# Attention's logits in four visits a half chunk instead of five, and two changes of order in the linear layers

## The chip, the cores and the metric

One Trainium2 chip, one of its NeuronCores. A core has five engines that run side by side and wait for each other through semaphores: TensorE (PE in the profile, with its weight loads as PEld), VectorE (DVE), ScalarE (ACT), GpSimd (POOL) and SyncE (SP), which only starts DMAs here. The metric is the time of one execution on the device, in microseconds, as the median of several runs.

## The reference

Four layers over `x` of 2048 tokens by 512 features, in float32: A, B, A, B, each with a layer norm ahead and a residual add behind. There are 32 heads of 16 features.

```python
def A(x):                        # linear attention with learned features
    q, k, v = heads(layernorm(x) @ wqkv)
    phi = lambda t: concat(softmax(t @ w_phi), softmax(-(t @ w_phi)))
    o = phi(q) @ (phi(k).T @ v) / (phi(q) @ phi(k).sum(0) + 1e-6)
    return x + merge(o) @ wo

def B(x):                        # softmax attention in 4 segments of 512, with a memory
    for s in range(4):
        p = softmax(qs @ ks.T * scale + causal_mask)
        o = g * (elu1(qs) @ M / (elu1(qs) @ z + 1e-6)) + (1 - g) * (p @ vs)
        M, z = M + elu1(ks).T @ vs, z + elu1(ks).sum(0)
    return x + merge(o) @ wo
```

## The kernel before

**Number format.** Most products with weights are made of three matmuls of a rounded high part and a low part of each operand (`mm3`: high by high, high by low, low by high). The low part is a subtraction on DVE (now and then on POOL) after ACT has copied the high part.

**Layer A** has two passes over the tokens. `pass1` walks four segments of 512 tokens in the order 1, 2, 3, 0 (`SEGS`). For each it normalizes, projects `v` (`v_tile`, 16 steps of three 512-wide matmuls), and then for four tiles of 128 tokens each makes keys (`kproj`) and queries (`qproj`). A key tile's features take `extremes` (DVE), `differences` (POOL), `exp` (ACT), and `scale_k` (DVE sums, then DVE and POOL multiply); `kv` sums the outer products of features and values on PE into `mx` and `my`. The value tiles of the next segment are steps of a plan that is woven into the projections of this one. In the last segment the queries stay on the chip: `begun(t)` does their extremes and differences. `pass2` goes over the 16 query tiles. For tile `i` it transposes the last output on PE (`turn`, split by ACT into `oh` and by DVE into `ol`), takes the exponential of tile `i + 2`, multiplies tile `i` with the state `KN`, divides (`weigh`, DVE), transposes tile `i + 1`, scales tile `i + 2` (`scale_q`: DVE sums and ratio `rr`, then POOL multiplies), makes the differences of tile `i + 3` (POOL) and projects tile `i - 1` with the output weights (`out_proj`, whose end is a DVE add into `x`, shown as `xr` or `ot`).

**Layer B** is a chain of 32 half chunks (4 segments, 4 chunks of 8 heads, 2 halves of 4 heads). `steps` walks a counter `k`; half chunk `m` has `R = 5` values of it, called visits 0 to 4 here. In every visit PE does, in this order: one part of the logits of half chunk `m` (`attend`, into `lg`, two banks of PSUM with one buffer), one part of the maxima's logits of a half chunk ahead (`maxima`, into the banks `mx` and `my`), in visits 0 and 2 one half of the products of the last half chunk's probabilities with the values (`weighted`, into a bank of its own, `pv`), and then background work from a table (`FIRST`, `GAPS`, `LAST`, `FINAL`): projections, memory, transposes and output projections, all through three banks called `g`. Visits 0 and 2 have no matmuls in the tables.

The logits contract over 63 or 64 rows, so each matmul uses one half of the array's rows (`tile_position` (0, 0) or (64, 0)), for one head pair `e` = 0 or 1. In the version before, each product is issued for `e = 0` and then for `e = 1` with the same width, so the two halves of the array always carry equal pairs. The products with the values use four column strips of 32 at once. Everything else uses the whole array. By width, a half chunk's `attend` is five visits with pairs of 512, 512, 256 + 384, 256 + 384 and 256 + 256 columns; `maxima` has five groups with pairs of 256 + 384, 512, 256 + 384, 256 + 256 and 512.

After `attend` ACT takes the exponential of the whole `lg` tile (1024 columns) into a `P4` tile, and POOL zeroes the masked part of the diagonal blocks. After `maxima` DVE adds the mask and takes the row maximum of each block (16 a half chunk, each followed by a read of its accumulator). ACT scales `pv` into `U`; POOL and DVE finish later.

**Order.** The order on every engine is the order of the program: the helper `held` chains PE's instructions, and `Ordered` those of the others. The table's "~" puts the DVE subtraction or add off to the next visit, behind that visit's maxima. The waits between engines come from tiles: a bank or buffer that is written anew waits for its last readers.

The profile gives all PE matmuls line L185 and all transposes L189 (helpers), and the other engines' operations L163.

Of the kernel before, what the change touches and what calls it, by code (L numbers as in the profile page):

```python
# [11 lines left out]
ALU = mybir.AluOpType  # L12
# [19 lines left out]
PV = 1  # L32
G = 3
R = 5
FILL = (1, 3, 4)
LEAD = 9
FINAT = 8
PAUSE, DONE = object(), object()
LEFT = 24900
BEGIN = -25  # L40
MAXIMA = -9
# [9 lines left out]

FIRST = """
0.1 max k2/2       | 0.2 v3/2          | 0.3 k2~
0.4 v3             | 1.1 max m0 q3/2   | 1.3 fin q3~       | 1.4 t1 k3/1
2.1 max m1 k3      | 2.3 fin ln~       | 2.4 ln~ ln~
3.3 fin q0+/2      | 3.0 w
3.1 max ln~        | 3.4 q0+~ t2
4.1 max k0+/2 load | 4.3 fin k0+/1     | 4.4 k0+ m2
5.0 n              | 5.3 fin q1+/2 n
5.1 max v0+        | 5.4 q1+~ t3  # L60
6.1 max a0+ v1+    | 6.2 n             | 6.3 a0+ fin k1+/2
6.4 k1+ m3         | 7.0 n             | 7.2 n
7.1 max q2+~       | 7.3 fin v2+/2 n   | 7.4 v2+ t0+
"""
GAPS = """
0.2 n              | 0.3 a1 fin v3/3 n
0.1 max a1 k2~     | 0.4 v3 turn~ m0
1.0 n              | 1.2 n
1.1 max q3~        | 1.3 fin out/2     | 1.4 out t1 turn~
2.1 max a2 m1 k3~  | 2.3 fin ln out/3  | 2.4 out turn~ ln  # L70
3.1 max ln ln out~ | 3.3 a2 fin q0+/2  | 3.4 q0+~ t2
4.1 max k0+~ a3 turn~ load | 4.3 a3 fin out/3 | 4.4 out~ m2
5.0 n              | 5.3 fin v0+/2 n N
5.1 max q1+~ begin | 5.4 v0+ t3
6.0 N              | 6.1 max a0+ k1+~  | 6.2 n
6.3 a0+ fin v1+/3 N | 6.4 v1+ m3       | 7.0 n N
7.1 max q2+~       | 7.2 n N           | 7.3 fin v2+/2 n N
7.4 v2+ t0+
# [3 lines left out]
0.1 max a1 k2~     | 0.2 n             | 0.3 a1 fin v3/3 n  # L82
1.0 n              | 0.4 v3 turn~      | 1.2 n
1.1 max q3~        | 1.3 fin out/2     | 1.4 out turn~
2.1 max k3~        | 2.3 fin a2 out/2  | 2.4 out a2 turn~
3.1 max ln~ ln~    | 3.3 fin out/2 ln~ | 3.4 out ln~ turn~
4.1 max v/2        | 4.3 fin out/2     | 4.4 out v
5.1 max v/2        | 5.3 fin v         | 5.4 a3 pre
6.1 max v/2        | 6.3 fin v a3      | 6.4 v/2 pt~
7.1 p v pt~        | 7.3 fin v/2 p pt  | 7.4 v p pt  # L90
"""
FINAL = """
0.1 max k2~        | 0.3 fin v3/3      | 0.4 v3 a1
1.1 max a1 q3/2    | 1.3 fin q3~       | 1.4 turn~
2.1 max k3/2       | 2.3 fin k3        | 2.4 out/2
3.1 max a2 out turn~ | 3.3 fin out/2   | 3.4 out~ a2
4.1 max a3 turn~   | 4.3 fin out/2     | 4.4 out/1 a3
5.1 max out turn~  | 5.3 fin out/2     | 5.4 out/1 pre
6.1 max out~       | 6.3 fin           | 6.4 pt~
7.1 p pt~          | 7.3 fin p pt      | 7.4 p pt  # L100
"""
BEFORE = {-25: "q0 load", -23: "v0", -21: "k0",
          -18: "n", -17: "v1 n", -16: "n", -15: "n n", -14: "q1 n", -13: "n", -12: "k1 n", -11: "n", -10: "v2 n",
          -4: "max q2~", -1: "t0"}
# [3 lines left out]
def interleave_kernel(ctx, tc, x_in, a_wqkv, a_wphi, a_wo, b_wq, b_wk, b_wv, b_wo, b_beta,  # L108
# [479 lines left out]
    class LayerA:  # L588
# [68 lines left out]
        def pass1(self, first):  # L657
# [35 lines left out]
            for n, s in enumerate(SEGS):  # L693
# [51 lines left out]
                if n < NSEG - 1:  # L745
# [5 lines left out]
                    plan += [(j, vt) for j in vals]  # L751
# [82 lines left out]
                begun(3)  # L834
# [9 lines left out]
        def pass2(self):  # L844
# [22 lines left out]
            for i in range(NT + 1):  # L867
# [5 lines left out]
                if i < NT:  # L873
# [24 lines left out]
                if 0 < i < 3:  # L898
                    yield from transposed(i + 1)
                x = ahead  # L900


    class LayerB:
        def __init__(self, xsrc, xdst):
            self.xsrc, self.xdst = xsrc, xdst
            self.st, self.hT, self.vv, self.ot, self.mx, self.U = {}, {}, {}, {}, {}, {}
            self.pr, self.pv = {}, {}
            self.later, self.late, self.rows, self.turned = [], [], [], []
# [109 lines left out]
        def maxima(self, m):  # L1018


            s, c, hf = m // 8, m % 8 // 2, m % 2
# [3 lines left out]
            def prod(pb, r, i, at, w):  # L1025
                for e in range(2):
                    q, k = Q[64 * e : 64 * e + 63, r, :], K[64 * e : 64 * e + 63, r, :]
                    mm(pb[e][:, at : at + w], lhsT=q[:, i * P : (i + 1) * P], rhs=k[:, 0:w],
                       start=True, stop=True, tile_position=(64 * e, 0))

            def top(pb, e, r, i, at):
                n = (i + 1) * P
                col = (e * 2 + r) * 4 + i
                pl = pb[e][:, at : at + n]
# [5 lines left out]
            for what in ([(0, 0, 0), (0, 2, P)], [(0, 3, 0)], [(1, 0, 0), (1, 2, P)],  # L1040
                         [(0, 1, 0), (1, 1, 256)], [(1, 3, 0)]):
                pb = [PS(t, 1) for t in ("mx", "my")]
                for r, i, at in what:
                    prod(pb, r, i, at, max(256, (i + 1) * P))
                for e in range(2):
                    for r, i, at in what:
                        top(pb, e, r, i, at)
# [12 lines left out]
        def attend(self, m):  # L1060


            s, c, hf = m // 8, m % 8 // 2, m % 2
# [3 lines left out]
            def prod(pb, r, kb, at, w):  # L1067
                for e in range(2):
                    q, k = Q[64 * e : 64 * e + 64, r, :], K[64 * e : 64 * e + 64, r, :]
                    mm(pb[:, e, at : at + w], lhsT=k[:, kb * P : (kb + 1) * P],  # L1070
                       rhs=q[:, 512 - w : 512], start=True, stop=True, tile_position=(64 * e, 0))

            for kbs, r in (((0,), 0), ((0,), 1), ((1, 3), 0), ((1, 3), 1), ((2,), None)):
                pb = PS("lg", 1, (P, 2, 512))
                pr = T2("P4", NP4, shape=(P, 2, 512))
                pq = pr.rearrange("p e (b x) -> p e b x", b=4)
                if kbs == (0,):
                    prod(pb, r, 0, 0, 512)
                    diags = [pr[:, :, 0:P]]
                elif kbs == (1, 3):  # L1080
                    prod(pb, r, 3, 256, 256)
                    prod(pb, r, 1, 0, 384)
                    diags = [pq[:, e, 0:4:3, :] for e in range(2)]
                else:
                    for rr in range(2):
                        prod(pb, rr, 2, 256 * rr, 256)
                    diags = [pr.rearrange("p e (r x) -> p (e r) x", r=2)[:, :, 0:P]]
                self.pr[m][kbs, r] = pr
                with tc.high_priority():
                    act.activation(pr, pb, AF.Exp, scale=0.25)  # L1090
                for diag in diags:
                    pool.affine_select(out=diag, in_=diag, pattern=[[0, diag.shape[1]], [1, P]],
                                            compare_op=ALU.is_ge, fill=0.0, base=0, channel_multiplier=-1)
                yield

        def weighted(self, m, last):
# [3 lines left out]
            if not last:  # L1100
                self.pv[m] = PS("pv", PV)
            pv, pr = self.pv[m], self.pr[m]
            for kb in ((1, 2) if last else (0, 3)):
                for r in range(2):
                    for e in range(2):
                        hh = 2 * r + e
                        h = c * 8 + hf * 4 + hh
                        if kb == 0:
                            p = pr[(0,), r][:, e, :]
                        elif kb == 2:  # L1110
                            p = pr[(2,), None][:, e, 256 * r : 256 * r + 256]
                        else:
                            p = pr[(1, 3), r][:, e, 0:384] if kb == 1 else pr[(1, 3), r][:, e, 384:512]
                        mm(pv[32 * hh : 32 * hh + 32, kb * P : 512],
                           lhsT=v[:, kb, h * VW : h * VW + 32], rhs=p,
                           start=(kb == 0), stop=(kb == 2), tile_position=(0, 32 * hh))
            if last:
                self.pr.pop(m)
                U = T2("U", 2)
                act.activation(U, self.pv.pop(m), AF.Identity, scale=share[:, m % 8 : m % 8 + 1])  # L1120
                self.U[m] = U

# [68 lines left out]
        def steps(self, side, after, table_end):  # L1191
# [75 lines left out]
            for k in range(BEGIN, R * N + 4):  # L1267
# [11 lines left out]
                if k % R in (0, 2) and 0 <= k // R - 1 < N:  # L1279
                    self.weighted(k // R - 1, k % R == 2)  # L1280
# [90 lines left out]
```

## Time and profile before

| what | value |
|---|---|
| median of three runs | 1522.89 us (1522.32 to 1524.72) |
| the profiled execution | 1523.71 us, span 1521.9 us |
| PE busy | 1456.3 us, 96% of the span |
| DVE busy | 1095.3 us, 72% |
| ACT busy | 787.1 us, 52% |
| POOL busy | 650.3 us, 43% |
| granted TensorE clock, mean | 0.995 |

Matmuls are pipelined: each is recorded for longer than it holds the array, so the records of neighbours overlap and PE looks busy through short stalls. What a matmul costs is read from the starts: the time from its start to the start of the next. A row of the timeline has the start, the length, the engine, the line, the operation, output and inputs with their shape, the count of merged instructions, and in brackets the idle time of the engine before it and what ended it.

### The profile page before, as it was taken

What the parts mean: (1) busy time and instruction counts of PE and PEld (TensorE: products, weight loads), DVE (VectorE), ACT (ScalarE), POOL (GpSimd) and SP (SyncE); (2) the same over time, 40 slices, a digit from 0 to 9 for tenths busy, and PEclk for the clock granted to TensorE, in tenths of its full rate; (3) what the DMA queues carried; (4) which work ended last, traced back from release to release, by engine and by line L of the source; (5) the groups of instructions that cost most, each with busy time, mean ns of one, the idle gap of its engine ahead of it and who ended that gap; (6) DMA issues with size and microseconds to landing.
All of it is one profiled execution on the core that took longest, in us unless ns stands there. A gap on an engine that the chain in (4) does not pass through costs nothing.

```text
span 1521.9 us, 30316 instructions
## 1 busy us (share of the span) xinstructions
PE 1456.3 (96%) x10888; PEld 1033.4 (68%) x10888; DVE 1095.3 (72%) x3258; ACT 787.1 (52%) x1178; POOL 650.3 (43%) x1000
## 2 busy tenths in 40 slices
PE   7999989999999999999999998999999999999998
PEld 6877767765666666666667786776656666666554
DVE  4765868668778877878656667757688788787783
ACT  5554335436565566556544333443565656655553
POOL 1668654313454544433314445541344445444331
PEclk9999999999999999999999999999999999999999
DMA  5487265545444443535340122744463353443340
GB/s 183 129 289 254 70 210 165 167 119 153 122 110 117 135 104 103 157 99 147 114 143 33 39 84 80 225 148 144 113 175 106 105 153 99 111 118 98 80 112 36
DMA packets 108773, 195.85 MB, mean 129 GB/s; under 512 B 14416, under 2 KB 27856, under 8 KB 107856
## 3 DMA queue, kind: packets, MB, share of 16 engines
q1 hardware_dynamic: 107472, 193.38, 42.8%
q8 instruction: 88, 1.44, 0.4%
q10 hardware_dynamic: 1152, 0.52, 0.1%
q14 instruction: 61, 0.50, 0.1%
HBM read 101.05 MB, written 39.85 MB: 93 GB/s over the span
## 4 chain that ended last, share of the span: by engine, by line
PE 78%; DVE 12%; ACT 4%; issue 2%; POOL 2%; DMA 1%; SPq 0%; ACTq 0%; POOLq 0%; DVEq 0%
PE g L185 45%; PE pv L185 9%; PE lg L185 9%; PE g L189 7%; PE mx L185 5%; PE my L185 3%; DVE mx L163 2%; POOL P L163 2%; DVE es L163 2%; ACT P L163 1%; DVE my L163 1%; DVE mxs L163 1%; ACT tb L163 1%; DVE hl L163 1%; DVE ol L163 1%
## 5 line engine op out<-in xcount | busy, mean ns | idle before, releaser
L163 ACT ACTIVATE P<-lg 128x1024 f32<-128x1024 f32 x320 | 328.9, 1028 | 173.0 <-PE lg L185 165.5
L163 POOL TENSOR_SCALAR_AFFINE_SELECT P<-P 128x256 f32<-128x256 f32 (+1 forms) x448 | 190.7, 440 | 442.3 <-ACT P L163 441.7
L163 DVE CUSTOM_DVE_ANT_0 mx<-mx,mask 128x128 f32<-128x128 f32 (+3 forms) x512 | 255.3, 499 | 160.7 <-PE my L185 109.0
L163 DVE CUSTOM_DVE_ANT_0 my<-my,mask 128x128 f32<-128x128 f32 (+3 forms) x512 | 265.9, 519 | 6.5
L185 PE MATMUL g<-hh,wqk 128*128 128x512 f32 x512 | 180.5, 407 | 2.1 <-ACT hh L163 1.4
L185 PE MATMUL lg<-e,e 64*128 64x256 f32 (+2 forms) x1024 | 168.4, 387 | 7.8 <-ACT P L163 7.6
L185 PE MATMUL g<-w,oh 128*128 128x512 f32 x512 | 170.6, 414 | 3.5 <-DVE ol L163 1.6
L185 PE MATMUL pv<-P,v 128*32 128x512 f32 (+3 forms) x2048 | 165.0, 441 | 0.0
L185 PE MATMUL my<-e,e 63*128 63x256 f32 (+2 forms) x512 | 146.7, 346 | 5.3 <-DVE mxs L163 3.9
L185 PEld LDWEIGHTS lg<-e,e 64*128 64x128 f32 x1024 | 81.1, 184 | 103.2 <-issue 50.6
L185 PE MATMUL g<-w,hh 128*128 128x512 f32 x448 | 145.8, 406 | 0.9 <-ACT tb L163 0.9
L163 DVE DVE_READ_ACCUMULATOR2_ANT mxs<- 128x1 f32 x1024 | 145.0, 142 | 0.0
L185 PE MATMUL mx<-e,e 63*128 63x256 f32 (+2 forms) x512 | 140.8, 330 | 0.2
L185 PEld LDWEIGHTS pv<-P,v 128*32 128x32 f32 x2048 | 53.7, 109 | 100.9 <-issue 92.0
L185 PEld LDWEIGHTS g<-hh,wqk 128*128 128x128 f32 x512 | 96.3, 188 | 24.0 <-ACT hh L163 1.8
L185 PEld LDWEIGHTS g<-w,oh 128*128 128x128 f32 x512 | 89.4, 190 | 30.9 <-issue 5.7
L185 PE MATMUL g<-w,ol 128*128 128x512 f32 x256 | 101.8, 398 | 0.0
L185 PE MATMUL g<-hl,wqk 128*128 128x512 f32 x256 | 100.4, 392 | 0.4 <-DVE hl L163 0.4
L163 POOL TENSOR_SCALAR tb<-tb 128x512 f32<-128x512 f32 x48 | 71.5, 1489 | 67.4 <-ACT tb L163 67.4
L163 ACT CAST ta<-g 128x512 fp32r<-128x512 f32 x64 | 37.6, 587 | 112.5 <-PE g L185 112.2
L185 PEld LDWEIGHTS my<-e,e 63*128 63x128 f32 x512 | 82.0, 185 | 18.1 <-DVE mxs L163 8.8
L185 PEld LDWEIGHTS mx<-e,e 63*128 63x128 f32 x512 | 89.7, 186 | 6.1 <-issue 3.6
(143 smaller groups left out, 2816.8 us busy)
## 6 DMA issues: line engine op xcount, KB each, us to landing
e<-ta SPq DMA_DIRECT2D x384, 128.0 KB
wqk<-wqk SPq DMA_DIRECT2D x64, 512.0 KB
x<-x SPq DMA_DIRECT2D x48, 256.0 KB
ot<-in SPq DMA_DIRECT2D x28, 256.0 KB
pq<-tb SPq DMA_DIRECT2D x24, 256.0 KB
tb<-pq SPq DMA_DIRECT2D x24, 256.0 KB
x<-xr SPq DMA_DIRECT2D x24, 256.0 KB
xr<-x SPq DMA_DIRECT2D x24, 256.0 KB
```

The source lines that it names most:

```text
L163: i = f(*a, **k)
L185: return held(nc.tensor.matmul(*a, **k))
L189: return held(nc.tensor.transpose(*a))
```

## The change

**Four visits (`R = 4`).** `attend` now has one visit for each pair (`r`, `e`). In it, head pair `e` gets its 512-wide product of key block 0, and the other pair `f = 1 - e` its 256-wide and 384-wide products of blocks 3 and 1; the array halves thus carry different widths, issued as `f` 256, `e` 512, `f` 384. Visits 2 and 3 add block 2 of pair `e` for both `r`: two 256-wide products into a new bank `mz`, with an exponential of their own. Per half chunk the matmuls are the same 16, the exponentials become six (four of 1024 columns, two of 512) instead of five, the mask operations ten instead of seven. `maxima` has four groups: three blocks (`f` 256, `f` 384, `e` 512) in two visits and five (two more 256-wide products of `e`, in `mz`) in the other two; visits 0 and 1 have the five. The 16 reductions stay. `weighted` does all 16 matmuls of a half chunk in visit 0, in one of the three `g` banks; the bank `pv` is gone and is now `mz`. The tables keep their cells, moved from visits 1, 3 and 4 to visits 1, 2 and 3; `LEAD`, `FINAT`, `BEGIN`, `MAXIMA` and `BEFORE` are moved to match, and the visits ahead of the first logits that have maxima alone are seven instead of nine.

**First linear pass.** For the last segment only, half of the 16 value steps stay in the plan of the segment before; the other eight are taken two by two after each of its four key projections (`rest`).

**Second linear pass.** `begun(3)` moves from the end of `pass1` into tile 0 of `pass2`. For each tile the differences of `i + 3` are issued ahead of the scaling of `i + 2`, and for the first three tiles the scaling moves to the end of the tile, behind the output projection.

```diff
-R = 5
+R = 4
...
-                    plan += [(j, vt) for j in vals]
+                    plan += [(j, vt) for j in (vals if n + 2 < NSEG else vals[::2])]
...
+                    rest = vt if n + 2 == NSEG else None
...
+                    for _ in range(2 if t < 4 else 0):
+                        next(rest)
+                        yield
...
-                begun(3)
+                self.begun = begun
...
-                    if i + 2 < NT:
-                        scale_q(self.e[i + 2])
+                    if i == 0:
+                        self.begun(3)
                     if i + 3 < NT:
                         self.e[i + 3] = differences(*self.raw.pop(i + 3))
+                    if 2 < i < NT - 2:
+                        scale_q(self.e[i + 2])
                     self.load_q(i + 4)
...
                 if 0 < i < 3:
                     yield from transposed(i + 1)
+                if i < 3:
+                    scale_q(self.e[i + 2])
...
-            for what in ([(0, 0, 0), (0, 2, P)], [(0, 3, 0)], [(1, 0, 0), (1, 2, P)],
-                         [(0, 1, 0), (1, 1, 256)], [(1, 3, 0)]):
+            for r, e, three in ((0, 1, True), (0, 0, False), (1, 1, False), (1, 0, True)):
                 pb = [PS(t, 1) for t in ("mx", "my")]
...
+                parts = [(pb[1 - e], 1 - e, r, 0, 0), (pb[1 - e], 1 - e, r, 2, P), (pb[e], e, r, 3, 0)]
+                if three:
+                    pz = PS("mz", 1)
+                    parts.insert(0, (pz, e, 0, 1, 0))
+                    parts.insert(2, (pz, e, 1, 1, 256))
...
+            for r in range(2):
+                for e in range(2):
+                    f = 1 - e
+                    pb = PS("lg", 1, (P, 2, 512))
...
+                    prod(pb[:, f, 256:512], f, r, 3, 256)
+                    prod(pb[:, e, :], e, r, 0, 512)
+                    prod(pb[:, f, 0:384], f, r, 1, 384)
+                    exp_of(pr, pb, pr[:, e : e + 1, 0:P], pr.rearrange("p e (b x) -> p e b x", b=4)[:, f, 0:4:3, :])
+                    if r > 0:
+                        pz = PS("mz", 1)
...
+                        for rr in range(2):
+                            prod(pz[:, 256 * rr : 256 * rr + 256], e, rr, 2, 256)
...
-            if not last:
-                self.pv[m] = PS("pv", PV)
+            pv, pr = PS("g", G), self.pr.pop(m)
+            for kb in (0, 3, 1, 2):
...
-                if k % R in (0, 2) and 0 <= k // R - 1 < N:
-                    self.weighted(k // R - 1, k % R == 2)
+                if k % R == 0 and 0 <= k // R - 1 < N:
+                    self.weighted(k // R - 1)
```

More of the change, by code (lines that the diff above doesn't have):

```diff
@@ L52 @@
 FIRST = """
[L53 to L63, printed above, removed]
+0.0 v3/2
@@ L79 @@
+7.3 v2+ t0+
 """
 LAST = """
[L82 to L90, printed above, removed]
+0.1 max a1 k2~ n   | 0.2 a1 fin v3/3 n
@@ L95 @@
[L95 to L100, printed above, removed]
-"""
-BEFORE = {-25: "q0 load", -23: "v0", -21: "k0",
-          -18: "n", -17: "v1 n", -16: "n", -15: "n n", -14: "q1 n", -13: "n", -12: "k1 n", -11: "n", -10: "v2 n",
-          -4: "max q2~", -1: "t0"}
+0.1 max k2~        | 0.2 fin v3/3      | 0.3 v3 a1
@@ L1023, in maxima, with prod @@
             mx = T2("mxs", 2, shape=(P, 16))
[L1025 to L1029, printed above, removed]
+            def prod(pb, e, r, i, at):
+                w = max(256, (i + 1) * P)
+                q, k = Q[64 * e : 64 * e + 63, r, :], K[64 * e : 64 * e + 63, r, :]
+                mm(pb[:, at : at + w], lhsT=q[:, i * P : (i + 1) * P], rhs=k[:, 0:w],
+                   start=True, stop=True, tile_position=(64 * e, 0))
             def top(pb, e, r, i, at):
@@ L1038, in top @@
                         op0=ADD, op1=MAX, accum_out=mx[:, col : col + 1])
-            for what in ([(0, 0, 0), (0, 2, P)], [(0, 3, 0)], [(1, 0, 0), (1, 2, P)],
-                         [(0, 1, 0), (1, 1, 256)], [(1, 3, 0)]):
+            for r, e, three in ((0, 1, True), (0, 0, False), (1, 1, False), (1, 0, True)):
                 pb = [PS(t, 1) for t in ("mx", "my")]
[L1043 to L1047, printed above, removed]
+                parts = [(pb[1 - e], 1 - e, r, 0, 0), (pb[1 - e], 1 - e, r, 2, P), (pb[e], e, r, 3, 0)]
[3 more added lines that the diff above has]
+                    parts.insert(2, (pz, e, 1, 1, 256))
+                for part in parts:
+                    prod(*part)
+                if not three:
+                    parts = [parts[i] for i in (0, 2, 1)]
+                for part in parts:
+                    top(*part)
                 self.mx[m] = mx
@@ L1065, in attend, with prod, exp_of @@
             self.pr[m] = {}
[L1067 to L1088, printed above, removed]
+            def prod(out, e, r, kb, w):
+                q, k = Q[64 * e : 64 * e + 64, r, :], K[64 * e : 64 * e + 64, r, :]
+                mm(out, lhsT=k[:, kb * P : (kb + 1) * P],
+                   rhs=q[:, 512 - w : 512], start=True, stop=True, tile_position=(64 * e, 0))
+            def exp_of(pr, pb, *diags):
                 with tc.high_priority():
@@ L1266, in steps @@
             spent = 0.0
-            for k in range(BEGIN, R * N + 4):
+            for k in range(BEGIN, R * N + 1):
                 m = k // R + 3
```

101 lines of the change are left out of this document (61 added, 40 removed).

## The prediction

> **What bounds the kernel now.** I read the page first (busy time, the chain that ended last), then the busy times of one stretch inside layer B, then the timeline of PE around single visits.
>
> ```profile
> PE 1456.3 (96%) x10888; PEld 1033.4 (68%) x10888; DVE 1095.3 (72%) x3258; ACT 787.1 (52%) x1178; POOL 650.3 (43%) x1000
> ...
> PE 78%; DVE 12%; ACT 4%; issue 2%; POOL 2%; DMA 1%; SPq 0%; ACTq 0%; POOLq 0%; DVEq 0%
> ...
> L163 DVE CUSTOM_DVE_ANT_0 mx<-mx,mask 128x128 f32<-128x128 f32 (+3 forms) x512 | 255.3, 499 | 160.7 <-PE my L185 109.0
> L163 DVE CUSTOM_DVE_ANT_0 my<-my,mask 128x128 f32<-128x128 f32 (+3 forms) x512 | 265.9, 519 | 6.5
> L163 DVE DVE_READ_ACCUMULATOR2_ANT mxs<- 128x1 f32 x1024 | 145.0, 142 | 0.0
> ```
>
> ```profile
> 340.00:700.00 360.00, 356.15 (x2637) 235.96 (x2636) 283.73 (x1020) 217.50 (x311) 159.90 (x287) 1.00 0.44 120
> ```
>
> The columns of the last row are the stretch, its length, and busy time of PE, PEld, DVE, ACT and POOL, then clock and DMA. PE is busy for 356 of 360 us and holds 78% of the chain; DVE follows with 284 of 360. So PE's order of work sets the time, and DVE is near enough to catch it for moments. What PE spends outside its streaming is in the starts:
>
> ```profile
> 701.83 0.40 PE L185 MATMUL g<-w,ol 128*128 128x512 f32 x1
> 702.16 0.50 PE L185 MATMUL lg<-e,e 64*128 64x256 f32 x4
> 702.50 0.28 PE L185 MATMUL mx<-e,e 63*128 63x256 f32 x1
> ...
> 702.62 0.27 PE L185 MATMUL mx<-e,e 63*128 63x256 f32 x1
> ...
> 702.82 0.73 PE L185 MATMUL g<-w,oh 128*128 128x512 f32 x2
> 703.39 0.40 PE L185 MATMUL g<-w,ol 128*128 128x512 f32 x1
> 703.62 0.64 PE L185 MATMUL g<-w,oh 128*128 128x512 f32 x2
> ...
> 705.32 0.50 PE L185 MATMUL lg<-e,e 64*128 64x512 f32 x2
> 705.66 0.40 PE L185 MATMUL mx<-e,e 63*128 63x512 f32 x1
> ...
> 705.99 1.28 PE L185 MATMUL pv<-P,v 128*32 128x512 f32 x16
> 707.21 0.50 PE L185 MATMUL lg<-e,e 64*128 64x512 f32 x2
> 707.55 0.28 PE L185 MATMUL mx<-e,e 63*128 63x256 f32 x1
> 707.68 0.39 PE L185 MATMUL my<-e,e 63*128 63x256 f32 x1
> 707.69 0.44 PE L185 MATMUL mx<-e,e 63*128 63x384 f32 x1
> 707.91 0.33 PE L185 MATMUL my<-e,e 63*128 63x384 f32 x1
> 708.17 0.28 PE L189 MATMUL g<-ident,mxs 128*16 128x128 f32 x1
> ...
> 710.24 0.46 PE L185 MATMUL my<-e,e 63*128 63x512 f32 x1 [0.20 <-DVE mxs L163]
> 710.63 1.28 PE L185 MATMUL pv<-P,v 128*32 128x384 f32 x16
> 711.85 0.56 PE L185 MATMUL lg<-e,e 64*128 64x256 f32 x4
> ...
> 712.73 0.44 PE L189 MATMUL g<-ident,U 128*128 128x128 f32 x2
> ```
>
> A full 512-wide matmul takes 0.23 us (703.39 to 703.62). Before a visit it takes 0.33 (701.83 to 702.16): 0.10 to change the shape of the array. The two pairs of `lg` take 0.34 (702.16 to 702.50), the next pair 0.12 (702.50 to 702.62): 0.10 is the first weight load, hidden by nothing. The last pair lasts 0.20 (702.62 to 702.82) instead of 0.12: 0.08 for leaving. The two full matmuls behind take 0.57 instead of 0.46. So a visit costs 0.40 us beside its streaming, half of it charged to the full-array work. By the same rows a pair of 512 streams 0.235 (705.32 to 705.66 is 0.34, less 0.105 for the load), a pair of 256 0.117, and a pair of 384 about 0.176 (between them, in proportion).
>
> **The change, part by part.**
>
> *Products with the values, all at once.* Two runs of 16 matmuls take 1.22 each (705.99 to 707.21, 710.63 to 711.85), 2.44 a half chunk. Each column strip streams 1280 columns in either run (512 + 128 twice, 384 + 256 twice), and that stays. No row splits a run into its streaming and the rest; the nearest is a visit's own share, 0.10 for the first load and 0.08 to 0.10 for leaving, so I take 0.20 of each run, and one of the two goes: 0.20 x 64 half chunks = 13 us. Ends: 0.10 (only the load, 6 us) and 0.30 (also the 0.10 of a change of shape, 19 us).
>
> *Four visits of logits instead of five.* The full-array runs stay three a half chunk, since visits 0 and 2 go straight from `pv` into the next `lg` (705.99 to 707.21). So the change to and from full array is paid as often as before; what goes is one first load and one leaving, 0.19. Against that stand unequal halves. Before, the equal pairs of a half chunk stream 2 x (2 x 0.235 + 2 x (0.117 + 0.176) + 2 x 0.117) = 2.58. After, each visit's longer half of the array has 512 + 512 + 256 + 256 columns, logits and maxima together (in visits 0 and 1 the 256s are maxima, in 2 and 3 logits): 0.70, and four of them 2.82. That holds if the halves run independently, which the rows of 707.68 allow: `my`'s 256 and `mx`'s 384 start as a pair, and `my`'s 384 starts 0.23 later, when a pair in step would have needed 0.105 + 0.176 = 0.28. So before 2.58 + 5 x 0.19 = 3.53, after 2.82 + 4 x 0.19 = 3.58: +0.05 x 64 = +3 us. Two visits with maxima alone go from each layer's start: -1 us.
>
> *Stalls inside visits.* By these prices the five visits should take 3.53; the visit of 707.21 took 0.96 (to 708.17) where 512, 256 and 384 give 0.72, because `my` waited for the reductions of the visit before. DVE needs 0.50 + 0.14 a reduction in the mean, so 1.3 to 2.6 us for a visit's two to four (the two of visit 0 are the widest), and visit 0 was over in 1.89 (705.32 to 707.21). After, five reductions (3.2 us) stand in visits 0 and 1. Visit 0 will last 0.90 + 2.24 = 3.1 us, and the wanted bank is asked for 0.4 later: the same thin margin as now, once, where before it came in two or three visits of five; visits 2 and 3 have 1.9 us of reductions in over 2.5. I take -0.1 a half chunk, -6 us. Ends: all such stalls gone, about 0.25 x 64 = -16 us (an estimate from the 0.24 seen here), and a new one of 0.3, +19 us.
>
> *Exponentials and masks.*
>
> ```profile
> L163 ACT ACTIVATE P<-lg 128x1024 f32<-128x1024 f32 x320 | 328.9, 1028 | 173.0 <-PE lg L185 165.5
> L163 POOL TENSOR_SCALAR_AFFINE_SELECT P<-P 128x256 f32<-128x256 f32 (+1 forms) x448 | 190.7, 440 | 442.3 <-ACT P L163 441.7
> ```
>
> ACT has 128 short exponentials in place of 64 long ones, POOL 192 more masks at under 0.44 us; both idle before this work (173 and 442 us), so nothing on the path. But their lead shrinks. `weighted` needed visit 4's results in visit 2 of the next half chunk; now it needs those of visit 3 right in visit 0, 0.9 us after its start. From the start of visit 3: products 0.6, exponentials 1.03 and less than 1.03, mask 0.44: 2.6 to 3.1 us. Visit 4 of this half chunk lasted 3.16 (702.16 to 705.32); with 0.23 for the longer visit and 0.9 for visit 0's logits the work has 4.3. Cost nothing; where a table cell is nearly empty, some tenths.
>
> *The bank of `pv` is a `g` bank now.* It is held from 0.9 in visit 0 until ACT has scaled it into `U`, some 0.7 after the run; visit 1's first transposes have the two others. Nothing, or 0.1 a half chunk (6 us) if a put-off DVE subtraction still holds one.
>
> *First linear pass.* Eight steps of 0.69 (three matmuls of 0.23) leave the plan of segment 3 of 4 and stand in the last one. PE does as much in all; what changes is cover:
>
> ```profile
> 130.38 0.73 PE L185 MATMUL g<-e,hh 128*128 128x512 f32 x2 [1.08 <-ACT tb L163]
> 140.90 1.97 PE L185 MATMUL mx<-P,v 128*64 128x64 f32 x60 [0.96 <-POOL P L163]
> ```
>
> In the emptied segment PE already waits twice for others, before the second query tile and before `kv`. One step fewer lies ahead of the first wait and two ahead of the second, so the waits grow by about 0.7 + 1.4: +2 us a layer, +4 in all (0 to +11, all 5.5 us of moved work uncovered twice). What it could give back is at the start of the second pass, next.
>
> *Second linear pass.*
>
> ```profile
> 198.78 1.06 ACT L163 ACTIVATE P<-P 128x1024 f32<-128x1024 f32 x1 [3.69 <-POOL P L163]
> 198.82 0.39 PE L185 MATMUL g<-w,ol 128*128 128x512 f32 x1
> ...
> 199.87 1.22 DVE L163 TENSOR_REDUCE es<-P 128x64 f32<-128x1024 f32 x1 [2.52 <-ACT P L163]
> ...
> 201.62 0.68 DVE L163 TENSOR_TENSOR xr<-g,xr 128x512 f32<-128x512 f32 x1
> ...
> 202.36 0.89 PE L189 MATMUL g<-ident,tmp 128*128 128x128 f32 x4 [2.27 <-DVE xr L163]
> ```
>
> The exponential waits for POOL's differences, which stand behind a scaling that waits for DVE; DVE's sums wait for the exponential, and the add `xr`, behind them in DVE's order, holds a `g` bank that PE's next transposes need: 2.27 us lost. With the scaling behind `out_proj`, `xr` follows the last matmul (198.82) after a few tenths, so this wait goes: -2.5 us a layer, -5 in all (0 to -12, if the other waits at this start go too). Tiles from 3 on keep their DVE order, and there I expect nothing.
>
> *Sum:* -13 + 3 - 1 - 6 + 4 - 5 = -18 us. The profiled execution took 1523.7 (span 1521.9), 0.8 over the median of 1522.9, which gives 1505 on the median's scale.
>
> **A rule weighed.** The rows first: pairs of 256 columns follow each other at 0.12 us on the same two halves (702.50 to 702.62) with a weight load for each, so a load hides behind a matmul on its own half. [...]
>
> **The rivals.**
>
> *The halves do not run apart* (by in-step pairs or by bare loads). If PE advanced in step, a visit's order of 256 | 512, 384 | 256, 256 | 384 and 512 would stream up to 0.76 instead of 0.70: 0.06 x 256 visits = 15 us, and 1520. [...] The start at 707.91 speaks against the former, the pairs against the latter. Together one chance in seven, mostly near 1520, which would mean that the change gives almost nothing.
>
> *All stalls in visits go* and the start of the second pass goes fully: 10 and 7 us more, 1488. For it: visits of 1.9 us, the tight ones, disappear. Against: DVE's 284 of 360.
>
> *Slower: visit 0 waits for its probabilities.* The place is the first `pv` matmul, behind which all of PE's order is queued. The point is a lead under 2.6 to 3.1 us; it decides once the wait averages 0.28 us a half chunk (18 / 64). If ACT or POOL came 0.6 late on average, the price is 38 us: 1543. Against it: ACT's idle 173 and POOL's 442 us; for it, that POOL's and ACT's other work stands in the same queues.
>
> **How the numbers follow.** The forecast has 0.56 (1495 to 1515), stalls gone 0.14 (1485 to 1495), halves not apart 0.15 (1515 to 1530, about a third of it within 3 us of no change), slower by waits 0.15 (above 1526). 0.2% is 3 us, about what a measurement tells from no change. Faster: 0.56 + 0.14 + 0.10 = 0.80; same 0.04; slower 0.16. The range goes from 1488 to 1526.
>
> **What would show it.** One run of 16 `pv` matmuls in a `g` bank per half chunk, about 2.2 us from its start to the next `lg`; `lg` to the first matmul behind the visit 0.90 us in all four visits; no idle time over 0.3 before `pv`; the wait for `xr` at 202 and 946 us gone; the two waits of the first pass longer. Wrong would be: visits of 1.0 us or more without a DVE wait (halves not apart), or PE's idle time before `pv` or a `g` bank of more than 18 us in sum.

## The result, and the profile after

The changed kernel takes 1562.1 us (median of four, 1561.08 to 1564.09) against 1523.81 for the kernel before beside it: a ratio of 1.0255, 95% interval 1.024 to 1.0271. It is 38 us slower where I forecast 18 us faster. The profiled execution took 1561.28 us with a span of 1559.5; the mean granted clock went from 0.995 to 0.984.

From the page of the changed kernel: busy times, the chain's shares, and the groups that answer to those shown of before.

```profile
PE 1456.1 (93%) x10888; PEld 1057.7 (68%) x10888; DVE 1054.0 (68%) x3258; ACT 776.5 (50%) x1242; POOL 675.9 (43%) x1192
...
PE 32%; DVE 6%; ACT 2%; issue 1%; POOL 1%; ACTq 0%; DVEq 0%; POOLq 0%
...
L163 POOL TENSOR_SCALAR_AFFINE_SELECT P<-P 128x256 f32<-128x256 f32 (+1 forms) x640 | 214.6, 363 | 442.0 <-ACT P L163 441.6
L163 ACT ACTIVATE P<-lg 128x1024 f32<-128x1024 f32 x256 | 263.2, 1028 | 147.0 <-PE lg L185 133.5
L163 DVE CUSTOM_DVE_ANT_0 my<-my,mask 128x512 f32<-128x512 f32 (+2 forms) x384 | 210.9, 549 | 78.2 <-PE my L185 78.1
```

PE is as busy as before in microseconds, in a span 38 us longer. (The chain's shares add up to 42% here, so they can't be set against the 78% of before.) ACT's and POOL's groups came out as counted, and no engine has become the bound: DVE is less busy than before. So PE waits. The list of PE's waits (bank, what it waited for, total us, times, longest us), first before, then after:

```profile
PE lg L185 <- ACT P L163: 7.6, 14, 1.4
...
PE g L185 <- ACT tb L163: 4.1, 7, 1.1
PE my L185 <- DVE mxs L163: 3.9, 14, 0.4
```

```profile
PE g L185 <- DVE ot L163: 9.8, 10, 1.9
PE g L185 <- ACT tb L163: 8.1, 9, 2.1
PE g L185 <- DVE wt L163: 7.2, 4, 1.8
PE g L185 <- DVE hl L163: 6.1, 9, 1.7
```

The waits for `lg` and `my`, inside visits, are gone from the top of the list. New ones stand for a `g` bank, the longest near 2 us each. Between the first and the last `lg` of the two layers B, PE's idle time ahead of matmuls into `g` went from 3.9 to 45.2 us in sum; more than 18 was one of my signs of being wrong. To find the place I took the start of the first `lg` matmul of every visit from the trace, 128 visits a layer. Visit 2 of the even half chunks in segments 1 and 2 lasts 5.3 to 7.5 us; the visit with the same cells lasted 4.0 to 4.3 before. One of them, visit 2 of half chunk 16 in the first layer B, PE, DVE and ACT of the changed kernel:

```profile
566.79 0.56 PE L185 MATMUL lg<-e,e 64*128 64x256 f32 x3
...
566.90 0.59 ACT L163 CAST ta<-g 128x512 fp32r<-128x512 f32 x1 [2.61 <-PE g L185]
...
567.69 0.30 DVE L163 CUSTOM_DVE_ANT_0 my<-my,mask 128x128 f32<-128x128 f32 x1 [1.41 <-PE my L185]
...
567.70 0.73 PE L185 MATMUL g<-mem,tb 128*128 128x136 f32 x4
...
567.90 0.73 DVE L163 CUSTOM_DVE_ANT_0 mx<-mx,mask 128x512 f32<-128x512 f32 x1
...
568.26 0.60 PE L189 MATMUL g<-ident,U 128*128 128x128 f32 x4
...
568.55 0.60 DVE L163 CUSTOM_DVE_ANT_0 my<-my,mask 128x384 f32<-128x384 f32 x1
...
569.07 0.68 DVE L163 TENSOR_TENSOR ta<-g,ta 128x512 fp32r<-128x512 f32 x1
...
569.79 1.08 ACT L163 ACTIVATE tb<-g 128x512 f32<-128x512 f32 x2 [0.88 <-DVE ta L163]
...
570.16 0.42 DVE L163 TENSOR_TENSOR ot<-g,r 128x256 f32<-128x256 f32 x1
...
570.73 0.70 PE L185 MATMUL g<-w,hh 128*128 128x512 f32 x2 [1.86 <-DVE ot L163]
...
571.58 1.05 PE L185 MATMUL g<-w,hh 128*128 128x512 f32 x2
...
572.43 0.63 PE L185 MATMUL g<-w,hl 128*128 128x512 f32 x1
...
574.27 0.79 PE L185 MATMUL lg<-e,e 64*128 64x256 f32 x3
```

The background of visit 1 ended in a key projection (`k2~`), whose bank ACT copies at 566.90 and from which DVE subtracts (`ta<-g,ta`). The "~" puts that subtraction behind the maxima of visit 2, and so it starts at 569.07, behind three reductions. Until then, and until ACT's two `tb` have read the same bank (to 570.87), it is held. PE meanwhile gives the second bank to `a1` (567.70) and the third to `fin` (568.26). DVE reads the second with `ot` (570.16 to 570.58), behind the same subtraction, and the third after that. So the projection `v3/3` stands without a bank from 568.9 to 570.73. Behind the wait the matmuls follow each other at 0.43 us instead of 0.23 (two of them from 571.58 to 572.43).

The same cells before the change, where they are split by visit 2's run of products with the values:

```profile
553.43 0.40 PE L185 MATMUL mx<-e,e 63*128 63x512 f32 x1
...
553.76 1.28 PE L185 MATMUL pv<-P,v 128*32 128x384 f32 x16
...
555.13 0.68 DVE L163 TENSOR_TENSOR ta<-g,ta 128x512 fp32r<-128x512 f32 x1
...
555.82 0.73 PE L185 MATMUL g<-mem,tb 128*128 128x136 f32 x4
555.85 1.09 ACT L163 ACTIVATE tb<-g 128x512 f32<-128x512 f32 x2
...
556.99 0.74 PE L185 MATMUL g<-w,hh 128*128 128x512 f32 x2
```

Here visit 2 has maxima (two reductions), 1.22 us of `pv`, which needs no `g` bank, and no background. The subtraction is over when visit 3's background begins, and the projection finds its bank with hardly any wait: ACT's `tb` ends at 556.94, PE starts at 556.99. My sum took that run away as overhead; it was also the cover of the put-off subtraction.

By the starts of the visits, layer B lasted 448.1 and 439.4 us before and 465.7 and 454.2 after (first to last `lg`): 32 us of the 38.

A second wait hides inside a row. Visit 0 of the same half chunk, with PE's weight loads (PEld), and the wait of such loads over the whole kernel:

```profile
559.36 3.16 PE L185 MATMUL g<-P,v 128*32 128x512 f32 x32
...
559.82 1.03 POOL L163 TENSOR_SCALAR_AFFINE_SELECT P<-P 128x128 f32<-128x128 f32 x3
...
560.18 0.19 PEld L185 LDWEIGHTS g<-P,v 128*32 128x32 f32 x6 [0.67 <-POOL P L163]
```

```profile
PEld g L185 <- POOL P L163: 11.8, 28, 1.1
```

The run of products with the values lasts 3.09 us here (to the next `lg` at 562.45) instead of 2.30, because POOL masks the probabilities only from 559.82 on. Ahead of these masks POOL worked on `tb` and `tmp`, from 556.34 on; it got `tb` late from ACT, and ACT waited for a put-off subtraction of DVE in the visit 2 before. By the starts of their matmuls, 15 of the 64 runs are stretched by 0.12 to 1.21 us, 11 us in sum (and the last run of the second layer, by 1.5, as in other versions too). PE's own list of waits doesn't show it, as its records of one run overlap.

The clock has a part in it: two stretches of 3 us behind waits of 2.07 and 2.05 us, and the whole of visit 2 above (stretch, length, busy times of PE, PEld, DVE, ACT, POOL, then the granted clock):

```profile
508.60:511.60 3.00, 3.00 (x19) 2.17 (x17) 0.83 (x3) 0.21 (x1) 2.92 (x3) 1.00 0.51 194
539.70:542.70 3.00, 3.00 (x12) 2.05 (x12) 0.50 (x2) 0.00 (x0) 2.47 (x3) 0.66 0.00 0
```

```profile
566.79:574.27 7.48, 5.62 (x27) 3.92 (x27) 3.42 (x12) 3.79 (x6) 4.47 (x6) 0.81 0.35 108
```

By the mean clock, 0.016 x 1559.5 = 25.0 us of clock are lost against 0.005 x 1521.9 = 7.6 before: at most 17 of the 38 us are the clock's, and less where PE would have waited anyway.

### The profile page after: what moved, and what is told of

It reads as the page before. It is cut to its first block, busy times and chain, and to the rows that moved or that the text cites. A ratio compares the mean times of both kernels' runs of the same rounds, so it can differ in the third digit from the quotient of the medians.

```text
span 1559.5 us, 30548 instructions
## 1 busy us (share of the span) xinstructions
PE 1456.1 (93%) x10888; PEld 1057.7 (68%) x10888; DVE 1054.0 (68%) x3258; ACT 776.5 (50%) x1242; POOL 675.9 (43%) x1192
## 5 line engine op out<-in xcount | busy, mean ns | idle before, releaser
L163 ACT ACTIVATE P<-lg 128x1024 f32<-128x1024 f32 x256 | 263.2, 1028 | 147.0 <-PE lg L185 133.5
L163 DVE CUSTOM_DVE_ANT_0 my<-my,mask 128x512 f32<-128x512 f32 (+2 forms) x384 | 210.9, 549 | 78.2 <-PE my L185 78.1
L163 DVE CUSTOM_DVE_ANT_0 mx<-mx,mask 128x128 f32<-128x128 f32 (+2 forms) x384 | 210.9, 549 | 74.2 <-PE mx L185 72.6
L163 DVE CUSTOM_DVE_ANT_0 mz<-mz,mask 128x256 f32<-128x256 f32 x256 | 115.0, 449 | 78.0 <-PE mz L185 41.3
L185 PE MATMUL g<-P,v 128*32 128x512 f32 (+3 forms) x2048 | 162.8, 439 | 1.2 <-DVE tb L163 0.5
L185 PEld LDWEIGHTS g<-P,v 128*32 128x32 f32 x2048 | 66.1, 110 | 82.8 <-issue 64.9
L185 PE MATMUL my<-e,e 63*128 63x512 f32 (+2 forms) x384 | 111.8, 344 | 2.3 <-DVE mxs L163 1.7
L185 PE MATMUL mx<-e,e 63*128 63x256 f32 (+2 forms) x384 | 112.7, 347 | 0.0
L185 PEld LDWEIGHTS g<-w,hh 128*128 128x128 f32 x448 | 80.5, 192 | 38.5 <-issue 14.1
L185 PE MATMUL mz<-e,e 63*128 63x256 f32 (+1 forms) x512 | 105.5, 286 | 0.0
```

What stands on the lines that cost most here:

```text
L163: i = f(*a, **k)
L185: return held(nc.tensor.matmul(*a, **k))
```

## The experiments

The theory after this reading: the loss is one put-off operation that holds a `g` bank, where the run in visit 2 had covered it. Rivals: the edits of the linear layers; the place of the products in a `g` bank; DVE late as a whole, by its five reductions a visit; the probabilities late, as in my slower rival. All times stand against the kernel before on the same chip, 1522.8 to 1524.3 us.

**Which part of the change.** The four visits alone:

```diff
 # the changed kernel, with all lines of pass1 and pass2 as before
-                    plan += [(j, vt) for j in (vals if n + 2 < NSEG else vals[::2])]
+                    plan += [(j, vt) for j in vals]
...
-                    if 2 < i < NT - 2:
+                    if i + 2 < NT:
                         scale_q(self.e[i + 2])
```

> The changed kernel with both edits of the linear layers undone: only the four visits stay. The theory: all of the loss is in layer B, where visit 2 of the half chunks with the cells "fin v3/3", "fin ln out/3", "fin q0+/2", "fin out/3", "fin v1+/3" waits some 2 us for a `g` bank and then runs at half clock for 3.4 us. Then this kernel takes 1553 to 1560, as the linear edits cost 2 to 9 by the trace of after. Rival, the linear edits gave the loss: 1524 to 1535. My prediction's terms: layer B alone at -17, about 1506.

Measured: 1561.48, ratio 1.0247 (1.0218 to 1.0277). The whole loss is the four visits' own. The two linear edits, each alone in the kernel before (their lines as in the change's diff):

> The kernel before with the edit of the first linear pass alone. My term was +2 us a layer, +4 in all (0 to +11). The trace of after has these waits longer by 0.75 + 0.4 + 0.7 us a layer, so +3 to +5: 1527 to 1529 against 1523.8. Rival, that the emptied segment is hidden: within 1 us of before.

> The kernel before with the edit of the second linear pass alone. My term was -5 (0 to -12), for the wait for `xr` that goes. The trace of after has that wait gone, but two others of 1.4 and 1.5 us at the start and a stretch at half clock. If those two belong to this edit: 0 to +3, 1524 to 1527. If they come from the first pass's edit: -5, 1519.

Measured: 1526.30 for the first pass, ratio 1.0024 (1.0014 to 1.0033), +3.5 us; 1519.41 for the second, 0.998 (0.9969 to 0.9991), -3.4 us. The rival of the linear edits falls: together they are worth nothing, each being near my term.

**One run of products with the values, five visits.**

```diff
 # the kernel before
-                if k % R in (0, 2) and 0 <= k // R - 1 < N:
-                    self.weighted(k // R - 1, k % R == 2)
+                if k % R == 0 and 0 <= k // R - 1 < N:
+                    self.weighted(k // R - 1, False)
+                    self.weighted(k // R - 1, True)
```

> The kernel before, with five visits, but both runs of products with the values in visit 0, in their own bank. It tells the saving of one run apart from the loss of the run that stood between the backgrounds of visits 1 and 3. Saving alone (my first term): -9 to -13, 1511 to 1515. If the run in visit 2 was what gave DVE time to empty the `g` banks, visit 3 now waits for banks as visit 2 of after does, by up to 1.2 us in the half chunks with the large cells, followed by half clock: -9 + 10 to 25, so 1524 to 1540.

Measured: 1584.53, ratio 1.0397 (1.0382 to 1.0413), above both expectations. The waits of this kernel say why:

```profile
PE lg L185 <- ACT P L163: 64.3, 73, 2.3
```

Visit 2 is empty now behind its logits, so the next visit asks for `lg` while ACT still has its 1.03 us exponential to do. The run also covered this, once a half chunk; the four visits avoid it, because each has either the products or background behind it. So this run shows that the second half was no mere overhead, but it doesn't test the bank.

**The order of the cells in visit 2.**

```diff
 # the changed kernel
-0.2 a1 fin v3/3 n
+0.2 v3/3 a1 fin n
...
-2.1 max a2 m1 k3~  | 2.2 fin ln out/3  | 2.3 out turn~ ln
+2.1 max a2 m1 k3~  | 2.2 out/3 fin ln  | 2.3 out turn~ ln
...
 # in the same way 3.2, 4.2 and 6.2, and 0.2 in the table LAST
```

> The changed kernel with the cells of visit 2 of the even half chunks in another order: the projection ("v3/3", "out/3", "q0+/2", "v1+/3") first, then "a1" and "fin". Theory (the pause is lost): visit 1's background leaves its last `g` bank to a put-off DVE subtraction that stands behind the maxima of visit 2; the short cells "a" and "fin" ask for two more banks within a microsecond, and the projection then finds all three held. With the projection first the third bank is asked for some 2 us later, so the waits of 1.8 to 2.1 us and the half clock behind them go: 16 places x 1.5 to 2.2 us = 24 to 35 us, so 1527 to 1538. Rivals: DVE is late in any order (five reductions in a visit): 1555 to 1562; the probabilities come late: no change, 1562.

Measured: 1530.43, ratio 1.0045 (1.003 to 1.0061). 31 us of the 38 are back by a change of places inside six cells, with the same work on every engine. Late probabilities, and DVE late whatever the order, fall as main causes. The stretched runs of visit 0 stay, with 11 us in sum.

**The put-off operations ahead of the maxima, in all visits.**

```diff
 # the changed kernel
                 put_off[0] = None
+                late, self.late = self.late, []
+                for f in late:
+                    f()
                 if -LEAD <= k < R * N - LEAD:
                     next(ma)
                 put_off[0] = None
-                late, self.late = self.late, []
-                for f in late:
-                    f()
```

> The changed kernel with the put-off DVE operations ahead of a visit's maxima instead of behind them, in all visits. Theory: the bank of the put-off subtraction comes free about 2 us earlier, so most of the waits in visit 2 go (-15 to -30), while the reductions start later and PE's own maxima wait by some 0.1 to 0.3 us a visit (128 visits a layer, +10 to +40): 1545 to 1575, with the waits for `g` small and those for `mx`, `my`, `mz` larger. Rival, the put-off operations don't matter: waits for `g` as in the changed kernel, 1562 or above.

Measured: 1511.42, ratio 0.992 (0.9906 to 0.9935): faster than the kernel before, and better than the theory had it. The reductions that start later cost some 8 us, by the run with visit 2 alone below.

**The products' bank by itself.**

```diff
 # the kernel before
-                self.pv[m] = PS("pv", PV)
+                self.pv[m] = PS("g", G)
```

> The kernel before, five visits and two runs of products with the values, but with these in one of the three `g` banks, held from visit 0 to visit 2. It measures what the lost bank costs by itself. My term for the change was 0 or +6, where the bank is held only through visit 0; here it is held through visit 1 as well, so that visit 1's background has two banks. If two banks are enough there: 1524 to 1527. If the third bank is what PE lacks: +0.3 to 0.7 us a half chunk, 1545 to 1570.

Measured: 1557.62, ratio 1.0228 (1.0212 to 1.0243), at a clock of 0.997. By the starts of the visits, visit 1 grew from 3.92 to 4.51 us in the mean of the first layer B and from 3.81 to 4.35 in the second, and the others stayed: 36 us over both for the lack of one bank through one visit of background, where the whole kernel lost 34. Three `g` banks are no comfortable number here. In the change the bank is held through visit 0 only, where the tables have next to no work, and visit 1 lasts 3.96 and 3.84 us in the mean there, near the 3.92 and 3.81 of before. So this price isn't the change's own.

**Useless work ahead of visit 2's background.**

```diff
 # the changed kernel, attend
-                    prod(pb[:, f, 256:512], f, r, 3, 256)
-                    prod(pb[:, e, :], e, r, 0, 512)
-                    prod(pb[:, f, 0:384], f, r, 1, 384)
+                    for _ in range(5 if (r, e, hf) == (1, 0, 0) and s in (1, 2) else 1):
+                        prod(pb[:, f, 256:512], f, r, 3, 256)
+                        prod(pb[:, e, :], e, r, 0, 512)
+                        prod(pb[:, f, 0:384], f, r, 1, 384)
```

> The changed kernel with useless work added: in visit 2 of the 16 even half chunks of segments 1 and 2 (both layers) the logits are computed five times over, 4 x 0.29 = 1.2 us more for PE ahead of that visit's background, 19 us in all. If the loss is a wait for `g` banks that DVE empties, the added work stands in the place of the wait and keeps the clock up: the wait of 1.8 to 2.1 us falls under 0.9 and the half clock goes, so the added 19 us are given back and more: 1545 to 1562, not slower than the changed kernel. If PE was simply busy, or waits for something that starts with these logits: 1578 to 1585.

Measured: 1581.17, ratio 1.0369 (1.0347 to 1.0392). Nothing is given back, so the theory in this form falls: time for DVE ahead of the background isn't enough. The same visit as above shows what was wrong with it:

```profile
571.06 1.46 PE L185 MATMUL lg<-e,e 64*128 64x256 f32 x13
...
572.57 0.40 PE L185 MATMUL mx<-e,e 63*128 63x512 f32 x1
...
573.03 0.73 PE L185 MATMUL g<-mem,tb 128*128 128x136 f32 x4
...
574.52 0.69 DVE L163 TENSOR_TENSOR ta<-g,ta 128x512 fp32r<-128x512 f32 x1
...
576.18 0.70 PE L185 MATMUL g<-w,hh 128*128 128x512 f32 x2 [1.98 <-DVE ot L163]
```

The added logits stand ahead of visit 2's maxima. DVE's reductions wait for these, and the put-off subtraction for the reductions: everything moved by the same amount, and the wait is 1.98 instead of 1.86. What counts is the time between the maxima and the background, which is where the run of `pv` had stood. (Work put behind the maxima wasn't tried.) That leaves the single operation put off into visit 2 as the cause.

**That operation alone.** As the order of all visits above, but only where `k % R == 2`; visits 0, 1 and 3 keep the put-off operations behind their maxima.

> The changed kernel with the put-off DVE operations ahead of the maxima in visit 2 alone; visits 0, 1 and 3 keep them behind. Theory, now narrower after the run with useless work: what holds the `g` bank is the one operation put off from visit 1 into visit 2, behind that visit's reductions. Then visit 2 alone gives most of what all visits gave (51 us): -35 to -50 against the changed kernel, 1512 to 1527. If the operations put off into visits 3 and 0 count as much: 1530 to 1550.

Measured: 1504.31, ratio 0.9866 (0.985 to 0.9883). Moving the put-off operation past three reductions, in one visit of four, takes 58 us off the changed kernel (by the differences to before, +38.3 and -20.0). Visit 2 of half chunk 16 in this kernel:

```profile
552.72 0.56 PE L185 MATMUL lg<-e,e 64*128 64x256 f32 x3
...
553.45 0.69 DVE L163 TENSOR_TENSOR ta<-g,ta 128x512 fp32r<-128x512 f32 x1 [1.21 <-ACT ta L163]
...
554.71 1.09 ACT L163 ACTIVATE tb<-g 128x512 f32<-128x512 f32 x2
...
555.86 0.73 PE L185 MATMUL g<-w,hh 128*128 128x512 f32 x2 [1.07 <-ACT tb L163]
...
558.13 0.56 PE L185 MATMUL lg<-e,e 64*128 64x256 f32 x3
```

The subtraction starts 0.73 us into the visit instead of 2.28, the wait is 1.07 instead of 1.86, the matmuls behind it keep their 0.23, and the visit lasts 5.41 instead of 7.48. What is left of PE's waits at this place is for ACT:

```profile
PE g L185 <- ACT tb L163: 16.1, 19, 1.2
```

In the means of the two layers visit 2 falls from 4.25 to 3.63 and from 4.11 to 3.52 us, 39 of the 58 us together. Visit 0 falls from 3.44 to 3.28 and from 3.49 to 3.35, 10 more: the stretched runs go too (the weight loads' wait for POOL's `P` falls from 11.8 to 2.4 us), so the masks were late by the same operation.

**The same order in the kernel before.** The edit of all visits, in the kernel with five:

> The kernel before with the put-off DVE operations ahead of the maxima in all visits. Theory: there visit 2 has a run of 16 products with the values, 1.22 us, between its maxima and the next background, which covers the reductions and the put-off operation, so the order gains nothing: 1523 to 1535, a loss where the reductions come later. Rival, the order of the put-off operations is worth some 10 us or more in either kernel, and the changed kernel had no special need of it: below 1515.

Measured: 1546.43, ratio 1.014 (1.0122 to 1.0158), a loss of 22 us and more than the theory had. With a cover in its place the put-off operation costs nothing behind the reductions: visit 2 lasts as long as before (2.03 and 2.02 us in the means of the two layers, now 2.02 and 2.02). Ahead of them it makes PE wait for the maxima's banks: visit 1 grows from 3.92 to 4.10 us in the mean of the first layer, visit 3 from 3.37 to 3.60. The waits of this kernel, beside 3.9 us in 14 before:

```profile
PE my L185 <- DVE mxs L163: 15.0, 64, 0.4
```

So "~" was right before the change and wrong after it, in visit 2 alone; in the other visits it is worth 8 us after the change (-12.0 against -20.0, each to the kernel before). The order of visit 2 alone wasn't tried in the kernel before.

**Together.** Both cures:

> The changed kernel with both cures: put-off operations ahead of the maxima, and the projection first in the cells of visit 2. With the former alone visit 2 of the even half chunks lasts 5.4 us, with the latter alone 4.7, the remaining waits being for ACT's `tb` (1.2 us) and for `ol`. If the two add up: 8 to 12 places x 0.7 us below 1511, so 1502 to 1507. If the waits only move to the later cells: 1508 to 1515.

Measured: 1498.34, ratio 0.9827 (0.9811 to 0.9844), a little better than added up. And a last kernel, with what each run had shown to be of use:

```diff
 # the changed kernel
 # put-off operations ahead of the maxima where k % R == 2
 # cells 0.2, 2.2, 3.2, 4.2, 6.2 with the projection first
-                    plan += [(j, vt) for j in (vals if n + 2 < NSEG else vals[::2])]
+                    plan += [(j, vt) for j in vals]
...
-                    for _ in range(2 if t < 4 else 0):
-                        next(rest)
-                        yield
```

> The changed kernel with put-off operations ahead of the maxima in visit 2 alone, the projection first in the cells of visit 2, and the edit of the first linear pass undone (that of the second is kept). By the runs so far: 1504.3 for the first; the cells gave 13 us on top of the other order (1511.4 to 1498.3), where the wait for `tb` in visit 2 fell from 15.8 to 3.5 us in sum, and the same wait has 16.1 us here; the first pass's edit cost 3.5 in the kernel before. If these add up: 1488 (1484 to 1495). If the cells' gain hung on the earlier reductions of the other visits: 1496 to 1502.

Measured: 1486.15, ratio 0.975 (0.973 to 0.977), 38 us under the kernel before. Its page and its list of waits:

```profile
PE 1426.0 (96%) x10888; PEld 1046.2 (70%) x10888; DVE 1055.2 (71%) x3258; ACT 775.8 (52%) x1242; POOL 673.3 (45%) x1192
```

```profile
PE g L185 <- ACT tb L163: 3.4, 7, 0.9
```

PE is 96% busy again, with the waits for `ot` and `wt` gone from the top of the list and that for `tb` at 3.4 us.

## Why the prediction was wrong

*Products with the values, all at once.* The failed step. The price of the run was near: 0.14 us saved a half chunk, not 0.20,

```profile
578.50 0.56 PE L185 MATMUL lg<-e,e 64*128 64x256 f32 x3
...
579.39 2.36 PE L185 MATMUL g<-P,v 128*32 128x512 f32 x32
581.69 0.56 PE L185 MATMUL lg<-e,e 64*128 64x256 f32 x3
```

2.30 from start to start, where nothing stretches the run, and two runs took 2.44, so -9 us instead of -13. But I took the run in visit 2 for pure cost and did not ask what was late without it. It stood between the maxima and the next background, and the put-off subtraction needed just that place: without it, PE's idle time for `g` banks in layers B rose by 41 us.

*The bank of `pv` is a `g` bank now.* Here I wrote the right mechanism beside the wrong visit: 6 us "if a put-off DVE subtraction still holds one". I looked at visit 1, whose banks are free in time. The subtraction that holds a bank is the one put off into visit 2, at up to 2.07 us a time, followed in seven places of twelve by a granted clock of 0.53 to 0.67 over 3 us; moving it is worth 58 us.

*Four visits instead of five.* The mechanism was right. The row part of a visit, from its first `lg` to the first matmul behind its maxima, takes 0.89 (578.50 to 579.39) where I had 0.90, so the two halves of the array do run apart with unequal widths. The shortest row parts add up to 3.57 us after (I had 3.58) and to 3.60 before (I had 3.53, as visit 3 takes 0.83 and not 0.72): -2 us instead of +3. No run shows a bare load for a matmul that follows another on the same half: in the changed kernel the shortest row parts of visits 2 and 3, which hold such sequences, are 0.89 us like those of visits 0 and 1, which by my prices is their streaming (0.70), one first load (0.10) and the leaving (0.09). So the rival that the halves do not run apart falls, with both its grounds.

*Stalls inside visits.* The size was wrong on the good side: summing, for each kind of row part, its time above the shortest of that kind, the two layers have 34 us before and 15 after, so -19 instead of -6, past the end of -16. The reductions hold PE up less inside the visits; it is the bank emptied behind them that does.

*Exponentials and masks.* "Cost nothing" was too low: 11 us, in runs of visit 0 that wait for POOL's masks. ACT's and POOL's idle time in sum (147 us, 173 before, and 442) did not show it, since the masks stood behind POOL's other work, the point that I had put down for the slower rival. That rival had the sign of the result, nearly the place and a part of the price, but not the cause: the masks come in time once the one DVE operation is moved.

*First and second linear pass.* +3.5 and -3.4 where I had +4 and -5. In the first layer the two waits grew by about half of what I said, by 0.38 (from 1.08) and 0.70 (from 0.96):

```profile
131.15 1.22 PE L185 MATMUL g<-e,hh 128*128 128x512 f32 x2 [1.46 <-ACT tb L163]
...
141.82 1.97 PE L185 MATMUL mx<-P,v 128*64 128x64 f32 x60 [1.66 <-POOL P L163]
```

In the second the wait for `xr` went, and another took over a part of it:

```profile
197.99 2.08 PE L185 MATMUL g<-KN,P 128*64 128x68 f32 x32 [1.43 <-ACT P L163]
```

That one belongs to this edit: in the kernel with it alone it lasts 1.68 us (at 194.58), and PE's waits between 184 and 207 us add up to 5.2 us where before they are 6.9.

*The sum.* With the one operation in its place the change is worth -20 us (1504.3). That this lies near the -18 of the forecast is luck, as the parts differ: in layers B -9 for the run, -2 for the visits, -23 for stalls in the visits (34 to 10 by the sum above), -6 for waits ahead of `lg`, +13 for waits for `g` banks (mostly ACT's `tb`) and +1 for stretched runs, together -26, where the two layers got 21 us shorter; 5 us stay unexplained. By the same count the changed kernel has -9, -2, -19 and -6 against +41 for `g` banks, +11 for stretched runs and, by an estimate from its trace, +14 for eight more stretches of half clock, 3.41 us each: +30 of the 32. My sum lacked one line, the work that had hidden behind the removed run.

## What to carry to other kernels

Work taken out of a full engine's order has two values: its own time, and the time that it gives to whoever frees the next buffer; the second is read by following the release of each bank that the next work asks for, not from the idle time of the engines. An operation that is deliberately put off is tied to what stands behind it at that moment, so after a change of rhythm each "put off" is to be looked at again. Where a few buffers feed mixed work, the order in which long and short work asks for them can be worth as much as the change itself: here 31 us.

## What the runs showed of the hardware

Behind some short waits the granted clock was lower. In the changed kernel's layers B twelve waits for a `g` bank lasted 1.80 to 2.07 us; behind seven of them the granted clock was 0.53 to 0.67 over the 3 us from half a microsecond after the wait, behind five it was 1.00. Waits of the same length are on both sides: behind the 1.80 us before 474.31 it was 0.67, behind the 1.80 us before 604.39 it was 1.00. Behind ten waits of 1.07 to 1.15 us in visit 2 of the kernel with the operation moved it was always 1.00, yet elsewhere a wait of 1.19 us (before 130.55 in the same kernel) was followed by 0.56, so the length of a wait alone doesn't tell.

In the changed kernel's clock record every stretch of half clock (0.50) that ends before the last matmuls lasts 3.41 us, but for one of 6.83 us. What sets off such a stretch these runs don't show.
